# Four products of each later block run on GpSimd in the loop, not on VectorE

## The chip, the cores and the metric

One NeuronCore of a Trainium2 chip runs the kernel. The metric is the device time in microseconds (us) of one execution. An execution with the profiler on has a time of its own and a span, from its first to its last instruction. In the profile PE is TensorE's matmul, PEld its weight load, DVE is VectorE, ACT is ScalarE, POOL is GpSimd and SP is SyncE, which issues most transfers (its queue is shown as SPq).

## What is computed

An attention block of the RWKV kind, and behind it two dense layers with x - tanh(x) between them. There are 4 x 8 heads with 768 tokens of 48 elements; the dense part sees 3072 tokens of 384 elements and 2048 hidden units.

```python
for t in range(S):                       # attention, S = 768
    cur = einsum('bhd,bhe->bhde', u * k[t], v[t])
    y[t] = einsum('bhd,bhde->bhe', r[t], state + cur)
    state = w[t][..., None] * state + einsum('bhd,bhe->bhde', k[t], v[t])
# (B,H,S,D) -> (B*S, H*D), then
h = x @ w_in
g = h - tanh(h)
out = g @ w_out
```

## The kernel before

The 768 tokens of each of the 4 batches are cut in two, so there are 8 blocks of 384 tokens, numbered 0 to 7. In a block the recurrence over tokens is replaced by chunks of 64 tokens: within a chunk, products of r and k with running products of the decays w turn it into matmuls (scores), and between chunks a state is carried on. Four pairs of heads lie on the 128 partitions; most steps work on half of the pairs, in the code `2` (pairs 2 and 3) and `0` (pairs 0 and 1).

A start-up (`boot`) makes the attention of block 0. Then the loop over blocks begins. While block i goes through the dense layers in 16 steps `f`, block i + 1 goes through its attention, and the first preparations of block i + 2 are made. A table (`plan`) says for each block at which step `f` which piece is issued. The loop writes out by hand the order of PE, SP, VectorE and ScalarE (`tc.manual_schedule(engines={PE, SP, DVE, ACT})`). GpSimd is not in that list: its instructions are put in order by the scheduler of the build.

The pieces that matter here, for the block that is prepared:

- `behind` (L429, VectorE) scans the decays of a chunk from its end and leaves the products in the tile `post`; a memset on GpSimd (L424) puts a one behind them.
- `take_whole` (L449, VectorE) reads one column of each chunk from `post`: the product over the whole chunk.
- `times_behind` (L443) multiplies the keys `k` with those products and writes the result over `post`, 768 elements per partition for a half. Then `earlier` (matmuls, L494), `split` (ScalarE, L542) and transposing transfers read `post`.
- `product_u` and `product_r` (L382, L386) take the keys by token, loaded by SP into the tile `k`, times `u` and then times `r`, 1152 elements per partition; `product_sum` (L390, VectorE) adds them up by head, and `diagonal_in` (L397) puts the sums on the diagonal of the scores.
- `before` (L417) and `times_before` (L436) do the like for `r`, on VectorE; `update` (L575, L587) makes the states.
- `together` (L757) makes the results of a block in four stretches of matmuls, two over states and two over scores, into two tiles. Both parts add into the same places, so the second part of a place must not begin before the first has ended. That is kept by a relay: a memset of one element on GpSimd waits for the first stretch, and the second waits for the memset (`begin_behind` adds such a wait):

```python
if first:
    ended[cross] = nc.gpsimd.memset(ended_at, 0.0)      # L764
    begin_behind(done, ended[cross])
```

- `result_out` copies the results to the columns `xT` for the dense layers of the next block, and `fill_holes` moves 16 rows of each by SP.

The dense layers are, per step `f`: `first` (L871, PE), `h` (L876, ScalarE), squares on ScalarE (L894 to L905), products and sums on VectorE (L879, L920, L1034), and the second layer on PE with sums of tiles formed ahead (L999), in the first and the last block in the plain form (L950, L977).

Behind the loop a branch redoes everything in a general form if a test on the values fails; with these inputs it isn't taken. That form calls `together` too, with another pool of PSUM tiles.

Of the kernel before, what the change touches and what calls it, by code (L numbers as in the profile page):

```python
# [46 lines left out]
ALU = mybir.AluOpType  # L47
# [4 lines left out]
P = 128  # L52
# [4 lines left out]
NCP = NCH // 2  # L57
# [4 lines left out]
UP = 2  # L62
HALVES = (UP, 0)
ALL = tuple(range(NPAIR))
D2 = 2 * D
DM = H * D
# [60 lines left out]
def kernel(  # L127
# [12 lines left out]
    nc = tc.nc  # L140
# [14 lines left out]
    u_row = const.tile([P, DM], F32, name="u_row", tag="u_row")  # L155
# [158 lines left out]
    def begin_behind(ins, then):  # L314
        tc.add_manual_dep(then.ins, ins.ins.name, mybir.DependencyInfo(
            mybir.DependencyClass.Sync, mybir.DependencyReason.DATA))
# [3 lines left out]
    class Block:  # L320
# [58 lines left out]

        def product_u(self, p0, n):  # L380
            t = self.by_token("k")
            nc.vector.tensor_tensor(out=t, in0=t, in1=u_row.unsqueeze(1).to_broadcast([P, NCP, DM]), op=ALU.mult)  # L382

        def product_r(self, p0, n):
            t = self.by_token("k")
            nc.vector.tensor_tensor(out=t, in0=t, in1=self.by_token("r"), op=ALU.mult)  # L386

        def product_sum(self, p0, n):
            src = self.by_token("k").rearrange("t c (p h d) -> t c p h d", p=NPAIR, h=2)
# [46 lines left out]
            return nc.vector.tensor_tensor(out=t, in0=self.tokens("r", p0, n).rearrange("d (c t) -> d c t", t=L),  # L436
                                           in1=t, op=ALU.mult)

        def times_behind(self, p0, n):


            t = self.half("post", p0, n * NCH * LP + 2)[:, 2:].rearrange("d (c j) -> d c j", j=LP)[:, :, 0:L]
            return nc.vector.tensor_tensor(  # L443
                out=self.half("post", p0, n * NB).rearrange("d (c t) -> d c t", t=L),
                in0=self.tokens("k", p0, n).rearrange("d (c t) -> d c t", t=L), in1=t, op=ALU.mult)

# [285 lines left out]
        def together(self, ps):  # L732

            self.results(ps)
            yp, spread, St, ended = self.yp, isinstance(ps, Kept), states[self.q], {}

            def scores(p, c, h, par):
                toks = slice(64 * par, 64 * par + 64)
                return self.v[toks, c, p * D2 + h * D:p * D2 + (h + 1) * D], A[toks, h, p, c, :]

            def from_state(p, c, h, par):
                rows = slice(64 * h, 64 * h + D)
                return St[rows, p, 2 * c + par, 0:D], self.chunk("pre", p, 2 * c + par, spread)[rows]

            def stretch(of, cross):
                first = cross not in ended
                begun = set()
                for n in range(UP):
                    for c in range(NCP):
                        for h in range(2):  # L750
                            for x in range(2):
                                p, par = UP * n + x, x ^ cross
                                if of is from_state and not (self.q or c or par):
                                    continue
                                lhs, rhs = of(p, c, h, par)
                                e0, n0 = 64 * (h ^ x), (n * NCP + c) * L
                                done = nc.tensor.matmul(yp[x][e0:e0 + D, par, n0:n0 + L], lhsT=lhs, rhs=rhs,  # L757
                                                        start=first and (x, e0) not in begun, stop=True,
                                                        skip_group_check=True)
                                begun.add((x, e0))  # L760
                                if not first and len(begun) == 1:
                                    begin_behind(ended[cross], done)
# [4 lines that stand above are left out]
            for of in (from_state, scores) if self.q else (scores, from_state):  # L767
                for cross in range(2):
                    stretch(of, cross)
            self.result_out(ALL)  # L770
            self.fill_holes([nc.sync])

        def fill_holes(self, engines, which=range(2 * KC)):
# [279 lines left out]
    def plan(i):  # L1053


        formed_w = {}
        if i == 0:
            phases = {6: ("turn",), 7: ("update",), 10: ("earlier",), 13: ("results",)}
            before = {0: ("behind 2", "take_whole 2"), 2: ("behind 0", "take_whole 0"), 3: ("times_behind 2",),
                      4: ("times_behind 0",), 5: ("before 2",), 6: ("before 0",), 7: ("times_before",),  # L1060
                      9: ("product_u", "held", "bound 2"), 10: ("product_r", "bound 0"), 11: ("product_sum",), 12: ("diagonal_in 2", "diagonal_in 0")}
            ahead = {}
            loads = {f: "weights" for f in (0, 1, 3, 4, 5, 6, 7, 8, 9, 10)}
            loads.update({2: "next r", 11: "w", 13: "k", 14: "r"})
            loads = {f: [name] for f, name in loads.items()}
            loads[3] += ["v", "row"]
            loads[4] += ["tokens k"]
            loads[9] += ["tokens r"]
        else:
            phases = {3: ("split 2 0",), 4: ("earlier", "split 2 1", "turned 2", "split 0 01"), 5: ("turned 0",),  # L1070
                      6: ("join 2 0",), 7: ("join 2 1",), 8: ("join 2 2",), 9: ("join 0 02",), 10: ("update",),
                      12: ("results",)}
            before = {0: ("times_behind 2",), 1: ("times_behind 0",), 3: ("times_before", "held"),
                      5: ("product_u",), 6: ("product_r",), 7: ("product_sum",), 8: ("diagonal_in 2",),
                      9: ("diagonal_in 0",)}
            ahead = {10: ("bound 2", "bound 0"), 11: ("behind 2", "take_whole 2"), 12: ("behind 0", "take_whole 0"),
                     13: ("before 2",), 15: ("before 0",)}
            loads = {1: ["v"], 3: ["tokens k"], 4: ["tokens r"], 7: ["w"], 9: ["k"], 11: ["r"]}
        if i == 1:
            phases = {4: ("split 2 0",), 5: ("split 2 1", "turned 2"), 6: ("split 0 01",),  # L1080
                      7: ("earlier", "turned 0", "join 2 0"), 8: ("join 2 1",), 9: ("join 2 2", "join 0 01"),
                      10: ("join 0 2",), 11: ("update",), 13: ("results",)}
            before = {0: ("behind 2", "take_whole 2", "bound 2"), 1: ("behind 0", "take_whole 0"),
                      2: ("times_behind 2",), 3: ("before 2", "bound 0"), 4: ("times_behind 0",), 5: ("before 0",),
                      6: ("times_before", "held"), 7: ("product_u",),
                      9: ("product_r", "product_sum", "diagonal_in 2"), 10: ("diagonal_in 0",)}
            ahead = {12: ("bound 2",), 13: ("behind 2", "take_whole 2"), 14: ("bound 0",)}
            loads = {1: ["v"], 4: ["tokens k"], 6: ["tokens r"], 9: ["w"], 11: ["k"], 12: ["r"]}
            formed_w = {2: (0, 1), 7: (2, 3, 4, 5), 9: (6,), 10: (7, 8), 11: (9,), 12: (0, 1), 13: (2, 3, 4, 5, 6),
                        14: (7, 8, 9)}  # L1090
        elif i == 2:
            phases.update({3: (), 4: ("split 2 0",), 5: ("earlier", "split 2 1", "turned 2", "split 0 01"),
                           6: ("turned 0", "join 2 0")})
            before = {0: ("behind 0", "take_whole 0", "times_behind 2"), 1: ("times_behind 0",), 2: ("before 2",),
                      3: ("before 0",), 4: ("times_before", "held"), 5: ("product_u",), 7: ("product_r",),
                      8: ("product_sum",), 9: ("diagonal_in 2", "diagonal_in 0")}
            loads = {1: ["v"], 3: ["tokens k"], 5: ["tokens r"], 8: ["w"], 10: ["k"], 11: ["r"]}
        return phases, before, ahead, loads, formed_w
# [6 lines left out]
    def more_weights(queue):  # L1105
        raws.append(load_weights(more_weights.n, queue))
        more_weights.n += 1
        return raws[-1][-1]
# [19 lines left out]
    def boot(ps, pair, blk, later):  # L1128
        h1, h2 = HALVES
# [12 lines left out]
        blk.totals_by_column(h1)  # L1142
        nc.scalar.copy(out=later_ident, in_=ident)
        blk.before(h1, UP)
        blk.times_behind(h1, UP)
        blk.times_u(h1, UP)
        own = blk.own(ps, h1, spare=94, ahead=5, late=6)
        blk.turn_1(ps, h1)
# [7 lines left out]
        blk.totals_by_column(h2)  # L1156
        blk.update_half(pair, h1)
        begin_behind(blk.done, more_weights(nc.sync))
        blk.times_behind(h2, UP)
        blk.times_u(h2, UP)  # L1160
        blk.turn_1(ps, h2)
        blk.turn_2(h2)
# [52 lines left out]
    with tc.tile_pool(name="ps_boot", bufs=1, space=PSUM) as ps_boot:  # L1215
        pieces = boot(Turns([scratch(ps_boot)] + ps_a.both), [hp] + acc, blocks[0], blocks[1])
# [156 lines left out]
    for op in ahead_of_h + rest:  # L1373
        op()
    nc.vector.tensor_single_scalar(again, sure[0:1, 0, 0:1], float(P * (n_whole + n_excess + n_top)),
                                   op=ALU.not_equal)
# [76 lines left out]
```

## Time and profile before

| | us |
|---|---|
| median of 3 runs | 544.39 (544.1 to 545.06) |
| the profiled execution, time | 545.07 |
| the profiled execution, span | 543.3 |
| PE busy | 534.1 (98%) |
| VectorE busy | 459.0 (84%) |
| ScalarE busy | 403.7 (74%) |
| POOL busy | 6.5 (1%) |

Busy time is the time in which the engine ran at least one instruction. A group of the profile is a line, its engine and operation, output and inputs with shapes, count, then busy us and the mean ns of one, then idle time of the engine just before it and what ended it. In a timeline the columns are the start in us, the duration in us, engine, line and operation; `x6` behind a row says that six like instructions are merged in it, and a bracket gives the idle time ahead of it and its releaser. A stage is a stretch of the span with the busy time of each engine in it.

### The profile page before, as it was taken

The page shows a single profiled execution, that of the slowest core. Times are in us where ns is not written, and L with a number is a line of the kernel's source. Part 1 is how long each engine was busy: PE and PEld are TensorE (multiplying, and loading weights), DVE is VectorE, ACT ScalarE, POOL GpSimd, SP SyncE. Part 2 cuts the span into 40 slices and gives each one's busy share as a digit, 9 for nine tenths or more (in the row PEclk, how much of TensorE's full clock was granted, in tenths as well). Part 3 has the DMA queues.
Part 4 walks back from the last instruction along what each step waited for, and adds up shares of the span by engine and source line. Part 5 has one row for each costly group of instructions (what it writes and reads, how often), then busy time and mean ns, then how long its engine had stood idle before and what let it go on. Part 6 is the DMA issues. An engine that isn't in the chain of part 4 may idle for free.

```text
span 543.3 us, 14866 instructions
## 1 busy us (share of the span) xinstructions
PE 534.1 (98%) x5682; PEld 403.3 (74%) x5682; DVE 459.0 (84%) x943; ACT 403.7 (74%) x814; POOL 6.5 (1%) x47
## 2 busy tenths in 40 slices
PE   7999999999999999999999999999999999999996
PEld 5756665678877777777887787877788788777874
DVE  7999999999989989798997979879797997557463
ACT  4899986888668876688767886688866885766561
POOL 1100000000000000000000000000000000000000
PEclk9999999999999999999999999999999999999999
DMA  7798732252311631154112532136321420100101
GB/s 276 234 402 311 259 119 74 97 137 63 122 42 54 162 118 57 43 147 119 60 56 87 122 103 70 48 97 151 84 89 46 122 27 3 56 1 0 45 1 46
DMA packets 53048, 56.34 MB, mean 104 GB/s; under 512 B 21488, under 2 KB 50928, under 8 KB 52976
## 3 DMA queue, kind: packets, MB, share of 16 engines
q1 hardware_dynamic: 52592, 55.18, 33.9%
q8 instruction: 48, 0.79, 0.6%
q14 instruction: 24, 0.20, 0.1%
q10 hardware_dynamic: 288, 0.10, 0.1%
q0 software_dynamic: 96, 0.07, 0.1%
HBM read 44.73 MB, written 4.72 MB: 91 GB/s over the span
## 4 chain that ended last, share of the span: by engine, by line
PE 88%; DVE 6%; ACT 2%; issue 2%; DMA 1%; SPq 0%; DVEq 0%
PE hp L871 41%; PE acc L999 27%; PE att L999 7%; PE att L757 4%; PE acc L950 3%; PE acc L977 2%; PE att L494 2%; PE att L575 1%; PE att L871 1%; ACT up L264 1%; DMA r<-in_rT 1%; DVE w_sb L268 1%; PE acc L871 1%; DVE scores L502 1%; DVE states L587 1%
## 5 line engine op out<-in xcount | busy, mean ns | idle before, releaser
L871 PE MATMUL hp<-xT,w_sb 128*128 128x384 f32 x738 | 259.3, 488 | 0.4 <-ACT h L876 0.4
L871 PEld LDWEIGHTS hp<-xT,w_sb 128*128 128x128 f32 x738 | 131.8, 190 | 70.0 <-ACT h L876 1.3
L999 PE MATMUL acc<-forms,g 128*128 128x128 f32 x954 | 133.2, 276 | 0.0
L876 ACT ACTIVATE h<-hp 128x384 f32<-128x384 f32 x123 | 60.3, 490 | 96.6 <-PE hp L871 96.5
L999 PEld LDWEIGHTS acc<-forms,g 128*128 128x128 f32 x954 | 122.0, 192 | 10.3
L879 DVE SCALAR_TENSOR_TENSOR h<-h,s 128x384 f32<-128x384 f32 x128 | 70.5, 551 | 51.9 <-ACT s L894 51.8
L920 DVE TENSOR_TENSOR g<-g 128x256 f32<-128x256 f32 x265 | 103.2, 418 | 7.4 <-PE acc L999 6.5
L895 ACT ACTIVATE qa<-s,shift 128x384 f32<-128x384 f32 x113 | 69.5, 615 | 3.7
L897 ACT ACTIVATE junk<-s,shift 128x384 bf16<-128x384 f32 x113 | 67.7, 599 | 0.0
L879 DVE SCALAR_TENSOR_TENSOR g<-qa,h 128x384 f32<-128x384 f32 x112 | 61.6, 550 | 1.6 <-ACT qa L905 0.2
L894 ACT ACTIVATE s<-h 128x384 f32<-128x384 f32 x113 | 59.2, 523 | 3.6
L999 PEld LDWEIGHTS acc<-w_sb,g 128*128 128x128 f32 x318 | 46.8, 191 | 9.7 <-ACT sums L967 0.3
L999 PE MATMUL acc<-w_sb,g 128*128 128x128 f32 x318 | 53.0, 276 | 0.0
L999 PE MATMUL att<-w_sb,g 128*128 128x128 f32 x212 | 35.5, 275 | 0.0
L999 PEld LDWEIGHTS att<-w_sb,g 128*128 128x128 f32 x212 | 31.1, 192 | 5.3
L1034 DVE TENSOR_TENSOR sums<-sums 128x256 f32<-128x256 f32 x84 | 32.8, 406 | 1.7 <-ACT sums L1011 1.4
L950 PE MATMUL acc<-w_sb,sums 128*128 128x384 f32 x96 | 33.9, 489 | 0.1
L264 ACT ACTIVATE up<-raw 128x768 f16<-128x768 f32 (+1 forms) x32 | 33.1, 1074 | 0.0
L950 PEld LDWEIGHTS acc<-w_sb,sums 128*128 128x128 f32 x96 | 17.9, 190 | 13.0 <-DVE sums L879 1.2
L417 DVE TENSOR_TENSOR_SCAN pre<-w,start 128x780 f32<-128x780 f32 x14 | 25.0, 1783 | 0.8
L429 DVE TENSOR_TENSOR_SCAN post<-w,seed 128x780 f32<-128x780 f32 x14 | 24.9, 1775 | 0.0
L897 ACT ACTIVATION_READ_ACCUMULATOR junk<-s,shift 128x1 f32 x113 | 21.1, 187 | 0.0
(118 smaller groups left out, 528.8 us busy)
## 6 DMA issues: line engine op xcount, KB each, us to landing
raw<-in_weights SPq DMA_DIRECT2D x16, 768.0 KB, 7.1
w<-in_wT SPq DMA_DIRECT2D x7, 780.0 KB, 4.7
k<-in_kT SPq DMA_DIRECT2D x7, 768.0 KB, 4.6
r<-in_rT SPq DMA_DIRECT2D x7, 768.0 KB, 4.6
v_sb<-in_v SPq DMA_DIRECT2D x8, 576.0 KB, 4.0
k<-in_tokens SPq DMA_DIRECT2D x7, 576.0 KB, 5.0
r<-in_tokens SPq DMA_DIRECT2D x7, 576.0 KB, 4.7
out_y<-sums SPq DMA_DIRECT2D x18, 128.0 KB, 1.8
```

Source lines behind the costliest of these rows:

```text
L264: return lambda: nc.scalar.activation(out=to, in_=of, func=AF.Copy, scale=scale, bias=bias)
L417: return nc.vector.tensor_tensor_scan(out=self.tile("pre")[:, cols], data0=self.tile("w")[:, cols], data1=start[:, 0:n * NCH * LP], initia ...
L871: nc.tensor.matmul(hp, lhsT=w_in_sb[:, f, kc, :], rhs=xT[kc], start=(kc == KC - 1), stop=(kc == 0))
L876: return h, nc.scalar.activation(out=h, in_=hp, func=AF.Copy, scale=1.0 / UPSCALE)
L879: return lambda: nc.vector.scalar_tensor_tensor(out=out, in0=in0, scalar=scalar, in1=in1, op0=op0, op1=ALU.mult)
L894: nc.scalar.activation(out=s, in_=h, func=AF.Square)
L895: nc.scalar.activation(out=qa, in_=s, func=AF.Square, bias=shift[:, 4:5])
L897: nc.scalar.activation(out=junk[:, 0:NB], in_=s, func=AF.Relu, bias=shift[:, 5:6], accum_out=excess[:, at:at + 1])
L920: return lambda: nc.vector.tensor_tensor(out=G[:, to:to + 2], in0=two(G, g_at(q, a0), g_at(q, a1)), in1=two(G, g_at(q, b0), g_at(q, b1)), ...
L950: nc.tensor.matmul(acc, lhsT=g[:, j * P:(j + 1) * P], rhs=w_out_sb[:, f, :], start=(f == self.first), stop=(f == NF - 1))
L999: nc.tensor.matmul(to, lhsT=G[:, g_at(q, a), :], rhs=rhs, start=start, stop=stop, skip_group_check=True)
L1034: ops.append(lambda op=op, at=at: nc.vector.tensor_tensor(out=at[0], in0=at[1], in1=at[2], op=OPS[op]))
```

## The change

In the loop, `times_behind`, `product_u` and `product_r` of blocks 1 to 7 are issued on GpSimd. The two `times_behind` of block 0, in the start-up, stay on VectorE. In the plan of block 1 `product_r` is issued at step 8, a step before `product_sum`. In the general form the copies of `result_out` are cut in two by partitions, 0 to 47 and 64 to 111; in the loop (`spread` true) they are as before.

```diff
         def product_u(self, p0, n):
             t = self.by_token("k")
-            nc.vector.tensor_tensor(out=t, in0=t, in1=u_row.unsqueeze(1).to_broadcast([P, NCP, DM]), op=ALU.mult)
+            nc.gpsimd.tensor_tensor(out=t, in0=t, in1=u_row.unsqueeze(1).to_broadcast([P, NCP, DM]), op=ALU.mult)
 
         def product_r(self, p0, n):
             t = self.by_token("k")
-            nc.vector.tensor_tensor(out=t, in0=t, in1=self.by_token("r"), op=ALU.mult)
+            nc.gpsimd.tensor_tensor(out=t, in0=t, in1=self.by_token("r"), op=ALU.mult)
...
-        def times_behind(self, p0, n):
+        def times_behind(self, p0, n, engine=nc.gpsimd):
...
-            return nc.vector.tensor_tensor(
+            return engine.tensor_tensor(
                 out=self.half("post", p0, n * NB).rearrange("d (c t) -> d c t", t=L),
                 in0=self.tokens("k", p0, n).rearrange("d (c t) -> d c t", t=L), in1=t, op=ALU.mult)
...
-            self.result_out(ALL)
+            self.result_out(ALL, None if spread else [nc.scalar.copy] * 2)
...
-                      9: ("product_r", "product_sum", "diagonal_in 2"), 10: ("diagonal_in 0",)}
+                      8: ("product_r",), 9: ("product_sum", "diagonal_in 2"), 10: ("diagonal_in 0",)}
...
-        blk.times_behind(h1, UP)
+        blk.times_behind(h1, UP, nc.vector)
...
-        blk.times_behind(h2, UP)
+        blk.times_behind(h2, UP, nc.vector)
```

## The prediction

> **What bounds the kernel now.** I read the page first: busy times, then the waits of PE, then the busy times by stage. The eight blocks (counted from 0) follow the start-up, from 23 us on, and most take some 64 us.
>
> ```profile
> span 543.3 us, 14866 instructions
> PE 534.1 (98%) x5682; PEld 403.3 (74%) x5682; DVE 459.0 (84%) x943; ACT 403.7 (74%) x814; POOL 6.5 (1%) x47
> PE hp L871 <- ACT h L876: 0.4, 1, 0.4
> ...
> 24.00:56.00 32.00, 31.62 (x180) 18.61 (x179) 29.56 (x52) 30.45 (x44) 0.00 (x0) 1.00 0.94 352
> ...
> 84.00:148.00 64.00, 64.00 (x653) 46.66 (x652) 62.27 (x125) 50.30 (x108) 0.58 (x5) 1.00 0.36 103
> ...
> 209.00:273.00 64.00, 64.00 (x707) 50.40 (x707) 55.70 (x115) 48.06 (x102) 0.32 (x4) 1.00 0.33 90
> ```
>
> The last three rows are stages: length, then busy us (with instructions) of PE, PEld, DVE, ACT and POOL. From 84 us on PE is busy 64.00 of 64.00 us in each block, at a granted clock of 1.00. VectorE is busier than the page's mean suggests, 62.27 of 64 in the second stage shown and 55.70 in the third, but PE waits for it nowhere that matters; the largest wait of a matmul in the loop is 0.4 us. So time taken off VectorE buys nothing where PE is full, and every microsecond for which PE is made to wait is added to the end. The whole question is whether the change makes PE wait.
>
> **What goes off VectorE.**
>
> ```profile
> L443 DVE TENSOR_TENSOR post<-k,post 128x768 f32<-128x768 f32 x16 | 15.2, 950 | 0.0
> L382 DVE TENSOR_TENSOR k<-k,u_row 128x1152 f32<-128x1152 f32 x7 | 9.4, 1344 | 0.0
> L386 DVE TENSOR_TENSOR k<-k,r 128x1152 f32<-128x1152 f32 x7 | 9.5, 1356 | 1.8 <-DMA r<-in_tokens 1.8
> ```
>
> Each of the seven later blocks loses two `times_behind` (0.95 us), one `product_u` (1.34) and one `product_r` (1.36) from VectorE: 4.6 us a block, 32.2 us in all (two of the 16 of L443 belong to the start-up, which stays). In a full PE that is worth 0. In the stage from 24 to 56 us PE lacks 0.38 us, which is the most that relief could give there.
>
> **What POOL gets, and in which order.** PE, SP, VectorE and ScalarE run in an order written out by hand; POOL isn't among them, and its queue is put in order by the scheduler of the build. In the built program of the changed kernel, both `times_behind` of each of the blocks 4 to 7 stand in POOL's queue ahead of the two one-element memsets `ended_at` (L764) that belong to the results of the block before; of block 3 one stands ahead of such a pair and one behind, and those of blocks 1 and 2 stand ahead of none. Those memsets are a relay: `together` sends the first half of its matmuls, a memset waits for them, and the second half on PE waits for the memset. So five times PE now waits for a queue in which a product stands first. That product cannot start early: it overwrites `post`, so it waits until `take_whole` (L449) has read it, on VectorE. Before, the relay cost nothing:
>
> ```profile
> 331.25 1.56 PE L757 MATMUL att<-pre,states 48*48 48x64 f32 x96
> 332.29 0.09 POOL L764 MEMSET ended_at<- 1x1 f32 x1 [10.93 <-PE att L757]
> 332.64 1.52 PE L757 MATMUL att<-scores,v_sb 64*48 64x64 f32 x96
> 333.52 0.17 DVE L449 TENSOR_SCALAR whole<-post 128x12 f32<-128x12 f32 x1
> ```
>
> (Columns: start, duration, engine, line.) The first half starts at 331.25; its 96 matmuls take 1.56 us, so the first group of 48 is done near 332.03, and the memset comes at 332.29: a hand-over of 0.26 us. The second half starts at 332.64, right behind the first. But `take_whole` of the half that the second product needs only runs at 333.52. In the changed kernel the memset stands behind a product that stands behind that row. The other four places have the same picture:
>
> ```profile
> 144.16 1.45 PE L757 MATMUL att<-pre,states 48*48 48x64 f32 x80
> 144.30 0.17 DVE L449 TENSOR_SCALAR whole<-post 128x12 f32<-128x12 f32 x1
> ...
> 204.78 1.52 PE L757 MATMUL att<-scores,v_sb 64*48 64x64 f32 x96
> 205.66 0.17 DVE L449 TENSOR_SCALAR whole<-post 128x12 f32<-128x12 f32 x1
> ...
> 268.74 1.46 PE L757 MATMUL att<-pre,states 48*48 48x64 f32 x80
> 269.24 0.17 DVE L449 TENSOR_SCALAR whole<-post 128x12 f32<-128x12 f32 x1
> ...
> 396.60 1.46 PE L757 MATMUL att<-pre,states 48*48 48x64 f32 x80
> 397.10 0.17 DVE L449 TENSOR_SCALAR whole<-post 128x12 f32<-128x12 f32 x1
> ```
>
> The wait of PE at each place is (end of L449 less start of PE's second half) + a hand-over 0.26 + the product's duration d + the memset 0.09 + a hand-over 0.26. The first terms are 144.47 - 144.16 = 0.31, 205.83 - 204.78 = 1.05, 269.41 - 268.74 = 0.67, 333.69 - 332.64 = 1.05 and 397.27 - 396.60 = 0.67: 3.75 us. Hand-overs and memsets: 5 x 0.61 = 3.05. Sum: 6.8 us + 5 d.
>
> **What d is.** No POOL row multiplies. The nearest are these:
>
> ```profile
> L171 POOL MEMSET start<- 128x780 f32 x1 | 0.8, 752 | 0.0
> masks.py:199 POOL TENSOR_SCALAR_AFFINE_SELECT ident<-ident 128x128 f32<-128x128 f32 x1 | 0.3, 283 | 0.0
> masks.py:197 POOL MEMSET ident<- 128x128 f32 x1 | 0.2, 205 | 0.3 <-POOLq L1445 0.3
> ```
>
> Writing costs (752 - 205) / (780 - 128) = 0.84 ns per element, so 768 written elements take 0.74 us; reading one operand adds (283 - 205) / 128 = 0.61 ns per element, 0.47 us for 768, twice. That estimate is 1.68 us. The floor is VectorE's own 0.95. Those POOL rows ran beside an idle VectorE; in the loop nearly every VectorE row reads two operands from the same memory, and no row shows POOL reading beside it. If reads took turns all the time, d would double to 3.4. I take 2.2, nearer to the end that POOL's own rows give. Sum: 6.8 + 5 x 2.2 = 17.8 us (11.6 at 0.95, 15.2 at 1.68, 23.8 at 3.4).
>
> **What else moves.** Of `product_u` and `product_r` nobody on PE waits directly; VectorE's `product_sum` does.
>
> ```profile
> 238.65 0.53 SPq L378 DMA_DIRECT2D r<-in_tokens  x1
> ...
> r<-in_tokens SPq DMA_DIRECT2D x7, 576.0 KB, 4.7
> ...
> 247.20 1.35 DVE L390 TENSOR_REDUCE diagonal<-k 128x24 f32<-128x1152 f32 x1
> ```
>
> The tokens of r land at 238.65 + 4.7 = 243.35; by the same arithmetic as above a 1152-element product takes 2.5 us on POOL, so it ends near 246.1 and L390 at 247.20 is not held: 0, with 1.1 us of cover. If POOL is twice as slow, L390 is some 1.4 us late. The load of the k tokens on SP and the copies of `split` on ScalarE now wait for POOL's products, which end earlier than VectorE's did (for blocks 4 to 7 they stand a step earlier): 0. In the plan of block 1 `product_r` moves a step forward in a queue that nothing else orders: 0. Splitting the copies of `result_out` in two concerns only the fallback behind the final branch, since `spread` is true in the loop: 0. PE's stall is not given back later: the columns of x that the next block needs are made after it, shifted with it, and PE has no idle time in which to catch up. VectorE, for its part, gains room from the stall.
>
> So the profiled execution (545.07 us, of which 543.3 span) would become 545.07 + 17.8 = 562.9; the median of the runs lies 0.68 lower, so I forecast 562 us.
>
> **The rivals.** First, whole instructions taking turns. If a POOL product that reads, and a VectorE row with two operands from SBUF, exclude each other for their whole length, `take_whole` comes later too.
>
> ```profile
> 264.73 1.77 DVE L429 TENSOR_TENSOR_SCAN post<-w,seed 128x780 f32<-128x780 f32 x1
> 266.54 0.17 DVE L449 TENSOR_SCALAR whole<-post 128x12 f32<-128x12 f32 x1
> 266.63 0.55 DVE L879 SCALAR_TENSOR_TENSOR h<-h,s 128x384 f32<-128x384 f32 x1
> 267.10 1.78 DVE L429 TENSOR_TENSOR_SCAN post<-w,seed 128x780 f32<-128x780 f32 x1
> 268.79 0.53 DVE L879 SCALAR_TENSOR_TENSOR g<-qa,h 128x384 f32<-128x384 f32 x1
> ```
>
> The first product becomes free at 266.71 + 0.26 = 266.97 and gets its turn at 267.10 for 1.7 us; the scan then runs from 268.8 to 270.6, L449 ends near 271.2, and the second product runs after the row in flight, from 271.6 to 273.3. PE goes on at 273.7 instead of 268.74: 5.0 us, 2.0 more than 0.67 + 0.61 + 1.7 = 3.0. Four such places give 8.0 and block 3 some 0.3 more: 15.2 + 8.3 = 23.5 us. Which of the two goes first changes little. Also, VectorE is held 2.5 us by each token product for the 1.35 us that it no longer spends, and it drifts 2.3 us late around 246 us, where a group that PE uses at 248.73 is ready just before:
>
> ```profile
> 245.98 1.30 DVE L920 TENSOR_TENSOR g<-g 128x256 f32<-128x256 f32 x3
> 248.73 1.05 PE L999 MATMUL acc<-forms,g 128*128 128x128 f32 x8
> ```
>
> 248.73 - 247.28 = 1.45 us of cover, so up to 0.9 us in each of six blocks, 5.4 us. This rival gives 568.6 to 574.0 by the profiled execution; I put it at 570. For it speaks that VectorE has few one-operand rows in this stretch, against it nothing in this trace, which has no overlap of the two. The Trainium skill ("SBUF — State Buffer", section "Who interferes with whom") states it as a rule: a VectorE instruction with two SBUF inputs contends with a GpSimd instruction that reads SBUF, and the one that comes second is blocked to the end of the first. No run here shows it yet; by that rule this rival's sum holds.
>
> Second, not slower: the wait vanishes if `take_whole` comes early enough. The point from which it decides: L449 must end 0.61 + 2.2 = 2.8 us before PE's second half, at 265.9 instead of 269.41, 3.5 us earlier. VectorE sheds 4.6 us a block, so if the shed rows had made it late here, the relay would be covered and the time would be 544.4, since PE is full. Against it:
>
> ```profile
> 259.24 0.56 DVE L879 SCALAR_TENSOR_TENSOR h<-h,s 128x384 f32<-128x384 f32 x1 [2.37 <-ACT s L894]
> ```
>
> At 259.24 VectorE had waited 2.37 us for ScalarE, after the last shed row of this block. What makes it late at 269 starts behind that point and isn't shed. The same wait stands ahead of the other places; in the stage from 84 to 148 us it is only short, so there the 3.1 us of its stall might shrink.
>
> Third, POOL may be much slower than I think, d = 4 us or more: 6.8 + 20 = 26.8, about 572 and up, without any exclusion.
>
> **How the numbers follow.** Forecast (d between 0.95 and 3.4, no exclusion of whole instructions) 0.52: 556 to 569. Exclusion 0.36: 568 to 574. Slower POOL 0.07: beyond 572. Relay covered 0.05: 544 or a little below. A measurement of this kernel tells some 0.2%, 1.1 us, from no change. Within the covered case the relief can give at most 0.4 us, so faster gets 0.02 for what I have not seen, no change 0.03, slower 0.95. The range from 555 to 574 leaves out the covered case and the far end of a slow POOL.
>
> **What would show it.** Right: a wait of PE's att L757 for POOL of about 3 to 4 us at four places and about 3 at one, none for blocks 1 and 2, and PE's busy sum unchanged at 534 us. d is read from the TENSOR_TENSOR rows on POOL. Exclusion would show as VectorE rows stretched or held beside a POOL product, above all the L429 scans, and as waits of PE's acc L999 for g. Wrong would be no wait of PE for POOL, or a loss spread over the blocks instead of in those five places.

## The result, and the profile after

The changed kernel takes 582.53 us (median of 4 runs, 580.07 to 583.27), the kernel before 544.54 in runs beside it (544.1 to 545.06): a ratio of 1.068 (95% interval 1.065 to 1.071), so it is slower by 38 us. Forecast were 562 us, in a range from 555 to 574. Direction and places were right, the size was half of what it is, and the range did not hold the time.

The page of the changed kernel, its profiled execution (581.84 us): span, busy times, and the TensorE clock that was granted, in tenths, in 40 slices of the span.

```profile
span 580.1 us, 14876 instructions
...
PE 547.2 (94%) x5682; PEld 411.7 (71%) x5682; DVE 474.3 (82%) x915; ACT 404.3 (70%) x814; POOL 83.8 (14%) x75
...
PEclk9999999999899997999979999999989999999999
```

Its waits of PE (total us, times, longest):

```profile
PE att L757 <- POOL ended_at L764: 19.9, 5, 4.4
PE acc L950 <- DVE sums L879: 2.8, 3, 1.7
...
PE att L494 <- DVE pre L436: 1.0, 1, 1.0
```

The span is 36.8 us longer (580.1 - 543.3). Three things are to be seen. PE waits five times for the relay, 19.9 us in all: the forecast had 17.8 in the same five places. PE is busy for 13.1 us more (547.2 instead of 534.1), although it runs the same 5682 matmuls; the clock line has four slices below 9, where that of before has none:

```profile
PEclk9999999999999999999999999999999999999999
```

And there are new waits for VectorE, 2.8 and 1.0 us. 19.9 + 13.1 + 3.8 = 36.8.

Where the three lie, the timeline of the second stall shows (start, duration, engine, line; a bracket is the idle time ahead and its releaser):

```profile
213.76 1.88 POOL L443 TENSOR_TENSOR post<-k,post 128x768 f32<-128x768 f32 x1 [9.76 <-DVE whole L449]
...
213.88 1.56 PE L757 MATMUL att<-pre,states 48*48 48x64 f32 x96
214.01 3.27 DVE L429 TENSOR_TENSOR_SCAN post<-w,seed 128x780 f32<-128x780 f32 x1
...
217.65 0.16 DVE L449 TENSOR_SCALAR whole<-post 128x12 f32<-128x12 f32 x1
217.95 1.76 POOL L443 TENSOR_TENSOR post<-k,post 128x768 f32<-128x768 f32 x1 [2.32 <-DVE whole L449]
218.10 2.02 DVE L879 SCALAR_TENSOR_TENSOR h<-h,s 128x384 f32<-128x384 f32 x1
219.65 0.23 POOL L764 MEMSET ended_at<- 1x1 f32 x2
...
219.79 2.81 PE L757 MATMUL att<-scores,v_sb 64*48 64x64 f32 x96 [4.35 <-POOL ended_at L764]
```

PE's first half ends at 213.88 + 1.56 = 215.44. Its relay memset stands behind the product of 217.95, that behind `take_whole` (L449) at 217.65, and that behind a scan that takes 3.27 us here and 1.77 alone in the kernel before. The scan ends at 217.28, 1.64 us behind the end of the POOL product that began just ahead of it, as if it had run only then; the L879 row beside the second product takes 2.02 us instead of 0.55. And the 96 matmuls behind the wait, which took 1.52 to 1.56 us, now take 2.81. The stages of 1 us around that place say why (length; busy us and instructions of PE, PEld, DVE, ACT, POOL; then the granted clock):

```profile
218.00:219.00 1.00, 0.00 (x0) 0.00 (x0) 1.00 (x2) 0.00 (x0) 1.00 (x1) 0.50 0.00 0
219.00:220.00 1.00, 0.21 (x8) 0.21 (x12) 1.00 (x1) 0.00 (x0) 0.83 (x3) 0.50 0.00 0
...
223.00:224.00 1.00, 1.00 (x3) 0.39 (x3) 0.96 (x1) 1.00 (x4) 0.00 (x0) 0.50 0.00 0
224.00:225.00 1.00, 1.00 (x4) 0.61 (x3) 0.00 (x0) 0.32 (x1) 0.00 (x0) 0.75 0.10 23
225.00:226.00 1.00, 1.00 (x8) 0.73 (x7) 0.00 (x0) 0.27 (x1) 0.00 (x0) 1.00 0.11 26
```

Within the wait the clock falls to 0.50, and after PE goes on at 219.79 it stays there to about 224.5, some 4.7 us, in which PE does half of its work. A stall of 4.35 us thus costs about 2.4 us more than its length. The Trainium skill ("TensorE: Matmul & The Clock Gate", "Part 1: The HAM clock gate") has a window of about 3.4 us, one idle such window for the clock to halve and one busy one for it to come back. Halving and return are seen here: the clock was at 0.50 from 217.68 to 224.50 us, 6.83 us, and in other stalls for 3.41. What length of wait sets it off was measured below.

The groups of the moved products and of two VectorE rows beside them (busy us, mean ns):

```profile
L443 POOL TENSOR_TENSOR post<-k,post 128x768 f32<-128x768 f32 x14 | 27.7, 1979 | 102.8 <-DVE whole L449 80.8 <-DVE w_sb L268 12.6 <-issue 9.4
L382 POOL TENSOR_TENSOR k<-k,u_row 128x1152 f32<-128x1152 f32 x7 | 20.7, 2963 | 169.6 <-DMA k<-in_tokens 169.6
L386 POOL TENSOR_TENSOR k<-k,r 128x1152 f32<-128x1152 f32 x7 | 29.1, 4159 | 48.1 <-DMA r<-in_tokens 25.6 <-issue 22.5
L429 DVE TENSOR_TENSOR_SCAN post<-w,seed 128x780 f32<-128x780 f32 x14 | 30.8, 2202 | 0.0
L879 DVE SCALAR_TENSOR_TENSOR h<-h,s 128x384 f32<-128x384 f32 x128 | 83.2, 650 | 63.9 <-ACT s L894 63.8
```

VectorE shed 32.2 us of products and is yet busier than before, 474.3 us instead of 459.0: the rows that are left take 47.5 us longer. L879 had a mean of 551 ns.

### The profile page after: what moved, and what is told of

Same layout as the page of the kernel before. It is cut to its first block, busy times and chain, and to the rows that moved or that the text cites. A ratio compares the mean times of both kernels' runs of the same rounds, so it can differ in the third digit from the quotient of the medians.

```text
span 580.1 us, 14876 instructions
## 1 busy us (share of the span) xinstructions
PE 547.2 (94%) x5682; PEld 411.7 (71%) x5682; DVE 474.3 (82%) x915; ACT 404.3 (70%) x814; POOL 83.8 (14%) x75
## 4 chain that ended last, share of the span: by engine, by line
PE 69%; DVE 20%; issue 8%; ACT 2%; POOL 0%; PEldq 0%; DVEq 0%; PEld 0%; POOLq 0%
PE hp L871 33%; PE acc L999 19%; PE att L999 6%; DVE states L587 3%; PE att L757 3%; DVE g L920 2%; DVE h L879 2%; PE acc L950 2%; DVE post L429 2%; PE acc L977 2%; DVE w_sb L268 2%; PE att L494 2%; DVE g L879 1%; DVE pre L417 1%; DVE s L902 1%
## 5 line engine op out<-in xcount | busy, mean ns | idle before, releaser
L871 PE MATMUL hp<-xT,w_sb 128*128 128x384 f32 x738 | 263.9, 494 | 0.0
L871 PEld LDWEIGHTS hp<-xT,w_sb 128*128 128x128 f32 x738 | 134.3, 194 | 71.6 <-issue 3.8
L879 DVE SCALAR_TENSOR_TENSOR h<-h,s 128x384 f32<-128x384 f32 x128 | 83.2, 650 | 63.9 <-ACT s L894 63.8
L920 DVE TENSOR_TENSOR g<-g 128x256 f32<-128x256 f32 x265 | 112.7, 454 | 7.1 <-PE acc L999 6.4
L879 DVE SCALAR_TENSOR_TENSOR g<-qa,h 128x384 f32<-128x384 f32 x112 | 67.5, 603 | 2.2 <-ACT qa L905 0.2
L382 POOL TENSOR_TENSOR k<-k,u_row 128x1152 f32<-128x1152 f32 x7 | 20.7, 2963 | 169.6 <-DMA k<-in_tokens 169.6
L443 POOL TENSOR_TENSOR post<-k,post 128x768 f32<-128x768 f32 x14 | 27.7, 1979 | 102.8 <-DVE whole L449 80.8
L386 POOL TENSOR_TENSOR k<-k,r 128x1152 f32<-128x1152 f32 x7 | 29.1, 4159 | 48.1 <-DMA r<-in_tokens 25.6
L729 ACT COPY late<-att 128x384 f32<-128x384 f32 (+1 forms) x9 | 4.3, 477 | 40.3 <-PE att L757 39.6
## 6 DMA issues: line engine op xcount, KB each, us to landing
v_sb<-in_v SPq DMA_DIRECT2D x8, 576.0 KB, 4.0
k<-in_tokens SPq DMA_DIRECT2D x7, 576.0 KB, 5.2
r<-in_tokens SPq DMA_DIRECT2D x7, 576.0 KB, 4.8
```

Source lines behind the costliest of these rows:

```text
L386: nc.gpsimd.tensor_tensor(out=t, in0=t, in1=self.by_token("r"), op=ALU.mult)
L871: nc.tensor.matmul(hp, lhsT=w_in_sb[:, f, kc, :], rhs=xT[kc], start=(kc == KC - 1), stop=(kc == 0))
L879: return lambda: nc.vector.scalar_tensor_tensor(out=out, in0=in0, scalar=scalar, in1=in1, op0=op0, op1=ALU.mult)
L920: return lambda: nc.vector.tensor_tensor(out=G[:, to:to + 2], in0=two(G, g_at(q, a0), g_at(q, a1)), in1=two(G, g_at(q, b0), g_at(q, b1)), ...
```

## The experiments

Two theories stood against each other. **Q**: the loss is the relay in POOL's queue, a stall of PE in five places, plus the half clock behind each stall, plus some 5 us in the first two stages, where VectorE is nearly full and the products hold it. **P**: the loss comes from the contention of POOL's products with VectorE's rows all over the loop, and the stalls of PE are only where it shows. All times are medians beside runs of the kernel before on the same chip.

**e1_relay_first.** The products stay on GpSimd; only their order in its queue is turned, behind the relay.

```diff
+            ins = engine.tensor_tensor(...)
+            if relay:
+                begin_behind(relay[-1], ins)
...
                     begin_behind(done, ended[cross])
+                    relay.append(ended[cross])
```

> The changed kernel, but each times_behind on GpSimd also waits for the last ended_at memset issued before it, so the relay of the results stands ahead of the products in POOL's queue. Theory Q (queue: the 38 us are 19.9 us of PE's wait for the relay, some 12 us of matmuls at half clock behind each of those waits, and 5 us of VectorE held beside POOL's products in the first two blocks): no wait of PE for POOL, granted clock 1.00, 549 to 552 us. Theory P (port: POOL's products and VectorE's two-operand rows shut each other out 28 times, some 1.3 us each, and the relay is only the place where that shows): 570 us or more, the wait turned into waits of PE for VectorE.

Measured: 550.24 us, ratio 1.012 (1.009 to 1.015). Its waits of PE (lines are up to five higher than in the kernel before):

```profile
PE acc L955 <- DVE sums L884: 2.8, 3, 1.7
...
PE att L498 <- ACT k L458: 1.4, 1, 1.4
PE att L498 <- DVE pre L437: 1.0, 1, 1.0
```

No matmul of the loop waits for POOL any more, PE is busy for 534.0 us, and 32.3 of the 38 us are gone (582.53 - 550.24), with each product still on GpSimd. Theory P, which expected 570 us or more, doesn't hold.

**e2_tokens_only** and **e3_behind_only** do one part of the change each: `times_behind` back on VectorE, or the two token products back.

```diff
-        def times_behind(self, p0, n, engine=nc.gpsimd):
+        def times_behind(self, p0, n, engine=nc.vector):      # e2
...
-            nc.gpsimd.tensor_tensor(out=t, in0=t, in1=u_row...
+            nc.vector.tensor_tensor(out=t, in0=t, in1=u_row...  # e3, product_r likewise
```

> The changed kernel with times_behind back on VectorE; product_u and product_r stay on GpSimd. Theory Q: the relay stands first in every block, so nothing of the wait and of the half clock is left; only the share of the two token products in the first blocks' 5 us: 545 to 549 us. Theory P: the two longer of the four products are left, some 20 us of the loss: about 563 us.

> The changed kernel with product_u and product_r back on VectorE; times_behind stays on GpSimd, in front of the relay as in the changed kernel. Theory Q: nearly the whole loss stays, 576 to 583 us, five waits of PE for POOL of 3 to 4.5 us and a clock near 0.976. Theory P: the two shorter of the four products are left, some 17 us: about 561 us.

Measured: e2 548.11 us, ratio 1.007 (1.005 to 1.008); e3 577.44 us, ratio 1.059 (1.057 to 1.062), with this wait:

```profile
PE att L757 <- POOL ended_at L764: 18.8, 5, 4.4
```

So the two `times_behind` of a block carry the relay's loss, and the token products, larger and slower on GpSimd, cost 3.6 us by themselves (548.11 - 544.49).

**e7_fill.** The changed kernel, with PE kept busy in the gap instead of idle: 14 matmuls of 128x128 that nobody reads, between the halves of `together`.

```diff
+                if spread and len(ended) == 2 and not filled and 2 <= self.b * NQ + self.q <= 6:
+                    filled.append(1)
+                    for _ in range(14):
+                        nc.tensor.matmul(hp[:, NB:BANK], lhsT=ident, rhs=ident, start=True, stop=True, ...)
```

> The changed kernel with 14 matmuls of 128 x 128 (some 3.1 us at full clock, results unused) ahead of the second half of together in the five blocks with a wait, so that PE works while it would wait. Theory Q, whose third part is the half clock behind a wait of 3 us or more: PE no longer idles that long, clock 0.995 or more, 568 to 572 us. If the clock falls for another reason than the idle PE: 0.976 as before and 582 us or more.

Measured: 571.06 us, ratio 1.048 (1.047 to 1.050). From its page and its waits:

```profile
PE 553.2 (97%) x5822; PEld 420.6 (74%) x5822; DVE 472.6 (83%) x915; ACT 404.3 (71%) x814; POOL 83.3 (15%) x75
...
PE att L758 <- POOL ended_at L765: 3.8, 5, 1.1
...
L774 PE MATMUL hp<-ident 128*128 128x128 f32 x140 | 17.0, 279 | 0.0
```

With 70 matmuls more (the profile counts each as two) it is 11.5 us faster than the changed kernel. Of PE's extra busy time, 553.2 - 534.1 = 19.1 us, the fill is 17.0. Behind the five places the half clock is gone: from the results of block 2 to those of block 7 the clock is 1.00. Of the wait 3.8 us are left. The clock fell once, to 0.72 from 40 to 46 us, behind a wait of 2.5 us for VectorE that the fill doesn't cover.

**e5_pad_short, e10_pad_three, e11_pad_four, e6_pad_long.** The kernel before, with all products on VectorE, and 2, 3, 4 or 5 memsets on POOL ahead of the first relay memset of blocks 2 to 6. Nothing is moved and nothing on POOL reads a tile; only the relay comes later.

```diff
                 if first:
+                    pads = 2 if spread and not cross and 2 <= self.b * NQ + self.q <= 6 else 0   # 3, 4, 5
+                    for _ in range(pads):
+                        pad = nc.gpsimd.memset(start, 0.0)
+                        begin_behind(done, pad)
                     ended[cross] = nc.gpsimd.memset(ended_at, 0.0)
                     begin_behind(done, ended[cross])
+                    if pads:
+                        begin_behind(pad, ended[cross])
```

> The kernel before, all products on VectorE, with two memsets of 128x780 on GpSimd (write only, estimated at 0.75 us each) ahead of the first ended_at memset in blocks 2 to 6: the relay to TensorE comes later by about 1.5 us in five blocks and nothing else changes. Theory Q (a wait of TensorE on the relay costs its own length, and half clock comes on top only behind the long waits, such as the changed kernel's of about 4 us each): five stalls of about 1.5 us, clock at 1.00, about 552 us (549 to 554). A rival, that the clock falls behind any wait on the relay: about 560 us or more, with the clock at 0.98. Theory P (what costs time in the changed kernel are products that hold VectorE, not TensorE's wait): at most 546 us.

> The same with five such memsets: the relay comes later by about 3.75 us in blocks 2 to 6, with no instruction on GpSimd that reads a tile. Theory Q: five stalls of about 4.1 us, 20 us together, and about 12 us of matmuls at half clock behind them: 573 to 579 us, the span's mean clock near 0.976, VectorE's rows as in the kernel before. If the stall alone counted (the forecast's sum): about 564 us at clock 1.00. Theory P: at most 548 us.

> As e5_pad_short with three write-only memsets: waits of TensorE of about 2.0 us in five blocks (1.2 with two memsets, 3.6 with five), 10 us together. Theory Q without a price for half clock at this length: about 555.5 us, clock 1.00. If the clock already halves behind 2 us (2.4 us extra for each): about 567 us, clock near 0.98. This run and the next say at what length of wait the second price begins.

> With four memsets: waits of about 2.75 us, 13.7 us together. Half clock behind them (2.4 us extra for each): about 571 us, clock near 0.975. Without it: about 559 us, clock 1.00.

Measured: 551.43 us, 1.012 (1.010 to 1.015), with two; 562.03, 1.032 (1.029 to 1.034), with three; 569.29, 1.045 (1.043 to 1.046), with four; 576.72, 1.058 (1.055 to 1.061), with five. Of each kernel, in this order, one fence with PE's busy time, its wait for the relay, and the 10 us behind one stall:

```profile
PE 534.4 (97%) x5682; PEld 403.5 (73%) x5682; DVE 459.5 (84%) x943; ACT 403.7 (73%) x814; POOL 14.0 (3%) x57
...
PE att L757 <- POOL ended_at L768: 5.9, 5, 1.2
...
207.00:217.00 10.00, 10.00 (x139) 7.54 (x139) 8.76 (x21) 6.08 (x14) 0.00 (x0) 1.00 0.22 62
```

```profile
PE 541.2 (97%) x5682; PEld 407.1 (73%) x5682; DVE 459.6 (82%) x943; ACT 404.5 (72%) x814; POOL 17.8 (3%) x62
...
PE att L757 <- POOL ended_at L768: 9.9, 5, 2.0
...
276.00:286.00 10.00, 9.77 (x117) 7.52 (x118) 6.03 (x14) 5.02 (x12) 0.21 (x3) 0.83 0.12 32
```

```profile
PE 545.7 (96%) x5682; PEld 411.3 (72%) x5682; DVE 459.8 (81%) x943; ACT 403.8 (71%) x814; POOL 21.5 (4%) x67
...
PE att L757 <- POOL ended_at L768: 13.9, 5, 2.8
...
282.00:292.00 10.00, 9.88 (x117) 7.76 (x118) 5.27 (x12) 5.16 (x12) 0.16 (x2) 0.83 0.13 34
```

```profile
PE 546.6 (95%) x5682; PEld 412.6 (72%) x5682; DVE 459.6 (80%) x943; ACT 403.8 (70%) x814; POOL 25.2 (4%) x72
...
PE att L757 <- POOL ended_at L768: 17.9, 5, 3.6
...
216.00:226.00 10.00, 9.84 (x133) 8.06 (x134) 4.85 (x11) 5.13 (x12) 0.18 (x2) 0.83 0.13 34
```

The five waits of such a kernel are alike, so their mean is a length (those of the change go from 3.3 to 4.4 us). The stretch from the results of block 2 to those of block 7 holds all five; the kernel before takes 316.33 us for it, with PE busy all the time.

| kernel | each wait | waits | PE busy above 534.1 | stretch above 316.33 | PE busy in it above 316.33 | median above before |
|---|---|---|---|---|---|---|
| two memsets | 1.2 | 5.9 | 0.3 | 6.9 | 1.0 | 6.6 |
| three | 2.0 | 9.9 | 7.1 | 17.6 | 7.7 | 17.4 |
| four | 2.8 | 13.9 | 11.6 | 24.6 | 10.6 | 24.6 |
| five | 3.6 | 17.9 | 12.5 | 29.2 | 11.2 | 31.9 |
| the change | 4.0 | 19.9 | 13.1 | 31.8 | 11.7 | 38.0 |

A wait of 1.2 us costs its length and 0.2 us. At 2.0 us a second price has come: in the stages behind the five stalls the clock was 0.83 at four and 1.00 at one. At 2.8 us all five show it, and from there it hardly grows, about 2.1 to 2.3 us for each stall (10.6, 11.2 and 11.7 over 5). What PE's busy time gained outside this stretch is no price of a stall: with four and five memsets the clock was 0.83 and 0.66 from 20 to 30 us, in the start-up, where it was 1.00 in the profile of before. The two expectations for three memsets were 555.5 and 567 us, and the run lies between them, on the edge.

Why one of the five stalls with three memsets kept its clock, the trace can tell in part. In the run with three memsets the starts of the stretches at half clock lie whole multiples of 3.41 us apart (147.31, 277.01, 345.28 and 413.55 us). Cut the trace into pieces of 3.41 us from there: of the stall from 208.09 to 210.07 us, which kept the clock, 1.3 us lie in one piece, of the others 1.6 to 2.0. Here is that piece, with PE busy for 2.09 us of it, and one behind which the clock fell, with 1.42:

```profile
208.75:212.16 3.41, 2.09 (x98) 1.00 0.00 0
...
273.60:277.01 3.41, 1.42 (x100) 1.00 0.02 5
```

(Of the engines only PE is in these two rows.) So the place of the wait in such a piece fits as the reason; no run set it.

In the stretch with the stalls the five memsets by themselves lose 29.2 us, the change 31.8, and VectorE is busy for 459.6 us with the memsets, as before: the relay's delay, and not what POOL reads, is the bulk of the loss. The other 5.0 us of the change's 36.8 lie ahead of that stretch.

**e8_later_first** and **e9_first_two** ask where the 5.7 us lie that e1_relay_first still loses (550.24 - 544.49). Both are e1_relay_first with the products of some blocks back on VectorE (where `times_behind` then waits for the relay too).

```diff
+            engine = nc.gpsimd if self.b * NQ + self.q >= 3 else nc.vector      # e8; e9: < 3
```

> As e1_relay_first (times_behind waits on GpSimd for the last ended_at memset), and the products of blocks 1 and 2 stay on VectorE; those of blocks 3 to 7 run on GpSimd. Theory Q (the 5.7 us that e1_relay_first still lost lie in the first two stages, where VectorE is busy nearly all the time and the products hold it): 544 to 546 us, clock 1.00. Rival (the products cost the same in every stage, by holding VectorE): five of seven stages keep their part, about 548.5 us. If VectorE's relief in blocks 3 to 7 were worth anything: under 543.5 us.

> The complement: only the products of blocks 1 and 2 run on GpSimd, those of blocks 3 to 7 on VectorE; times_behind behind the relay as in e1_relay_first. Theory Q: nearly all of that kernel's loss, 549 to 551 us, with the later blocks' stages at the lengths of the kernel before. Rival (the same cost in every stage): about 546 us.

Measured: e8 545.51 us, ratio 1.0006 (0.9989 to 1.0022), no difference; e9 550.10 us, ratio 1.010 (1.007 to 1.012), nearly the whole rest. From the results of block 3 (210.96 us) to those of block 7 (466.68) e9 takes 255.72 us, just what the kernel before takes (203.39 to 459.11). In e8 the groups on POOL read:

```profile
L389 POOL TENSOR_TENSOR k<-k,r 128x1152 f32<-128x1152 f32 x5 | 23.3, 4667 | 24.7 <-DMA r<-in_tokens 24.7
L448 POOL TENSOR_TENSOR post<-k,post 128x768 f32<-128x768 f32 x10 | 18.1, 1822 | 9.5 <-DVE whole L457 8.9
```

A `product_r` of 4.67 us, 3.4 times its time on VectorE, costs nothing in blocks 3 to 7, and VectorE's relief there brings nothing.

**e12_write_only.** e9_first_two, with each product on GpSimd replaced by memsets of its output.

```diff
+            if engine is nc.gpsimd:
+                for _ in range(3):
+                    engine.memset(t, 0.0)
+                return
```

> As e9_first_two, but each product of blocks 1 and 2 on GpSimd is left out and three write-only memsets of its output (0.75 us each for 128x768, estimated 1.1 us each for 128x1152, so no shorter on GpSimd than the products alone) stand in its place: the outputs are not the reference's. VectorE is relieved of the same products and the next steps wait for GpSimd in the same way; only the reads of tiles by GpSimd are gone. Theory Q (instructions on GpSimd that read hold VectorE's two-operand rows): 543.5 to 546 us, L888's mean back near 0.55 us. Rival (the loss of e9_first_two comes from steps that wait longer for GpSimd): 549 to 551 us.

Measured: 544.57 us, ratio 0.999 (0.998 to 1.000). Here are the stages from 30 to 50 and from 50 to 70 us of the kernel before, of e9 and of e12, and after them the L879 group of e9 (L888) and of e12 (L902), and e9's waits of PE for VectorE:

```profile
30.00:50.00 20.00, 19.62 (x68) 11.57 (x68) 18.87 (x35) 18.75 (x27) 0.00 (x0) 1.00 1.02 390
50.00:70.00 20.00, 20.00 (x229) 12.37 (x228) 19.35 (x38) 20.00 (x31) 0.13 (x2) 1.00 0.64 217
```

```profile
30.00:50.00 20.00, 17.83 (x59) 10.19 (x58) 18.85 (x31) 19.07 (x27) 4.69 (x2) 1.00 1.02 385
50.00:70.00 20.00, 19.73 (x234) 12.55 (x233) 19.31 (x33) 17.43 (x26) 3.85 (x1) 1.00 0.58 199
...
L888 DVE SCALAR_TENSOR_TENSOR h<-h,s 128x384 f32<-128x384 f32 x128 | 74.3, 581 | 49.4 <-ACT s L903 49.4
...
PE acc L959 <- DVE sums L888: 3.0, 3, 1.7
...
PE att L502 <- DVE pre L439: 1.0, 1, 1.0
```

```profile
30.00:50.00 20.00, 19.61 (x69) 11.58 (x68) 17.17 (x31) 18.61 (x27) 4.43 (x6) 1.00 1.04 399
50.00:70.00 20.00, 20.00 (x229) 12.32 (x228) 19.20 (x41) 20.00 (x30) 6.49 (x8) 1.00 0.67 226
...
L902 DVE SCALAR_TENSOR_TENSOR h<-h,s 128x384 f32<-128x384 f32 x128 | 70.7, 553 | 57.2 <-ACT s L917 57.2
```

With POOL busy for 10.9 us in the two stages (8.5 in e9), but reading nothing, L902 is back at 553 ns, PE at 19.61 of 20, and the loss is gone. So the last 5 us come from GpSimd's reads, which hold VectorE where it has no room: from 30 to 50 us it needs 18.85 us in e9 for 31 rows, and 17.17 in e12 for as many, and PE, which lives on them, lacks 1.8 us (19.61 - 17.83). In all, PE waits 4.0 us for VectorE in e9's first two stages, waits that neither the kernel before nor e12 has. One more thing differs in e12: without its read of `r`, the stand-in of block 1's `product_r` comes at 53.53 us, and not at 71.66. That doesn't save the rival: from 24 to 150 us nothing waits for one of POOL's products in e9. (The profiled execution of e9 also had a clock of 0.83 from 10 to 30 us, ahead of these stages; that is not part of this loss.)

With e6 and e12 the rule that the prediction cites from the Trainium skill ("SBUF — State Buffer", "Who interferes with whom") is borne out on both sides: reads on GpSimd block VectorE's two-operand rows, writes alone don't.

## Why the prediction was wrong

**The bound, and relief worth nothing: right.** PE is full, and e8, with 4.6 us a block off VectorE in five blocks, is at 1.0006 of the kernel before.

**The queue order and the five places: right.** Five waits for the relay, none for blocks 1 and 2; turning the order alone (e1) takes 32.3 us away.

**The sum of the waits, 17.8 us: near (19.9), partly by errors that cancel.** In the stall of the timeline above, d was 1.76 us and not 2.2; POOL's own memset rows had given 1.68. The hand-overs and the memset took 219.79 - 217.81 - 1.76 = 0.22 us, not 0.61. But L449 ended 217.81 - 215.44 = 2.37 us behind PE's need, not 1.05, since the scan ahead of it was held by the first product. That is the mechanism of the exclusion rival: it had the right rows. For the place at 268.74 us its stall was 5.0 us, and 3.98 were measured, since it put 0.4 us ahead of the second product and 0.4 behind it where 0.15 and 0.09 were needed (L449 ends at 288.16, the product runs from 288.31 to 290.07, PE goes on at 290.16).

**"PE's busy sum unchanged at 534 us": the step that failed.** The forecast took a microsecond of waiting as a microsecond lost, since the granted clock was 1.00 in every stage of before. That trace has no wait of 2 us in the loop, so it could not show what one does to the clock. What the runs showed in its place is a clock of 0.50 for 3.4 or 6.8 us around each stall: PE was busy for 547.2 us, and the missing term is 13.1 us, 11.7 of them in the stretch with the stalls. It was missing from every rival as well, so the range was too low as a whole: 562.9 + 13.1 = 576.0 for the forecast, and 570 + 13.1 = 583.1 for the exclusion rival. That the last comes so near to 582.53 is in part luck, since its stalls were too long.

**"0" for the token products and for VectorE's drift: failed in the first two stages, right in the others.** The forecast gave L390 a cover of 1.1 us, from a product of 2.5 us. POOL's product took 4.16 us in the mean, since back-to-back VectorE rows hold it just as it holds them. That costs nothing in blocks 3 to 7 (e8). In the first two stages, where VectorE was busy for 29.56 of 32 and 62.27 of 64 us, it cost some 5 us with the products of `times_behind` (e9 less e12, 550.10 - 544.57, is 5.5). The prediction had quoted both rows, and read them only for what relief could bring there, not for what a hold would cost. The exclusion rival put up to 5.4 us on it, but in six later blocks.

## What to carry over

Before work is moved to an idle engine, list what already stands in that engine's queue and who waits for it: here a one-element memset, cheap and late, carried TensorE's progress, and two products that stood ahead of it cost 32 of the 38 us. Price a wait of a full TensorE by its length plus the slow clock behind it, and ask whether it can be kept short or filled. Where VectorE has no room, products on GpSimd that read don't relieve it: in the changed kernel its other rows grew by 47.5 us for the 32.2 taken away.

## What was not expected of the hardware

- A wait of TensorE of 1.2 us for the relay left the granted clock at 1.00; one of 2.0 us halved it for some time in four of five cases, and waits of 2.8 us and more in five of five, at 2.1 to 2.3 us of extra matmul time each. The Trainium skill ("TensorE: Matmul & The Clock Gate", "Why this matters for your kernels") asks for no idle gaps over about 3 us; here the edge lay between 1.2 and 2.0 us for the waits for the relay. It isn't the wait's length alone: in the first stage of the changed kernel a wait of 1.7 us for VectorE left the clock at 1.00.
- Filling a wait with matmuls that nobody reads made the changed kernel faster by 11.5 us.
- The hold is not for rows with two operands alone. L465, with one input tile, takes 0.17 us in the kernel before; beside `product_r` of block 1, from 68.98 us on, it took 2.69 us.
- The hold goes both ways. A GpSimd product of 1152 elements took 5.28 us beside a row of VectorE instructions, and VectorE then waited for it:

```profile
261.10 5.28 POOL L386 TENSOR_TENSOR k<-k,r 128x1152 f32<-128x1152 f32 x1 [4.18 <-DMA r<-in_tokens]
...
266.41 1.35 DVE L390 TENSOR_REDUCE diagonal<-k 128x24 f32<-128x1152 f32 x1 [2.52 <-POOL k L386]
```
